# Attention scores as one fp32 product on two row tiles instead of three products of high and low parts

## The chip, the cores and the metric

The kernel runs on one core of a Trainium2 chip, in one launch. The metric is device time in microseconds; the median of the runs of a kernel counts. The engines of the core are named as the profile names them: PE (TensorE matmuls, with its weight loads as PEld), DVE (VectorE), ACT (ScalarE), POOL (GpSimd) and SP (SyncE, which issues the transfers). They run side by side, each works through its own instructions in the order of the program, and semaphores hold an instruction until what it reads is there.

## What is computed

Three parts follow each other: attention in which each query keeps its 32 best keys, a dense two-layer block, and a mixture of eight experts of which each token visits one. The attention has 2 batches, 8 heads, 576 tokens and 64 elements per head. Shortened:

```python
scores = scale * np.matmul(q, k.transpose(0, 1, 3, 2))
kth = np.partition(scores, -top_k, axis=-1)[..., -top_k:-top_k + 1]
scores = np.where(scores >= kth, scores, -1000000000.0)
attn = np.exp(scores - max); attn = attn / (attn.sum + 1e-09)
x = attn @ v                        # then heads side by side: 1152 x 512
h = x @ w_in                        # 512 x 2048, float64 as it comes
x = (h * np.tanh(softplus(h))) @ w_out
expert_idx = argmax(xn @ en.T / tau)
out[mask] = gate_w * (np.maximum(x[mask] @ w1[e], 0.0) @ w2[e])
```

Which 32 keys are kept, and which expert a token visits, hang on comparisons, so the scores must be good to about fp32.

## The kernel before

**Attention** is cut into 36 steps. A step (`attention_step`, p from 0 to 35) takes 128 query rows of two heads (a pair of heads, hp), or, for the last 64 rows of a batch (i = 4, steps 16 to 19), 64 rows of four heads. A step does this, in order: PE transposes the queries (tile pq), ACT copies them to SBUF (qT); PE makes the scores in two halves of 288 keys (tile ps, two units n = 0 and 1, one PSUM buffer of two banks between them), ACT copies each half to sp; DVE finds the 32 largest (eight MAX8 for each row set over 72 keys each into cand, then MAX8 and MATCH_REPLACE8 on cand); ACT counts; DVE or POOL makes the part below (e); DVE takes its maxima; ACT makes exponentials; DVE makes the threshold kths; POOL or DVE masks; PE transposes the masked exponentials (pt) and ACT copies them; PE multiplies with the values (pv); DVE or ACT normalises into x.

**High and low parts.** A query or key is split into two fp32r numbers: the high part is a copy into fp32r (ACT, or POOL by `copy_pool`), the low part is the fp32 number less the high part (POOL, or DVE in batch 0's first pieces). Queries: `queries`, tiles qn and qs. Keys: `keys` for the first 512 keys of a pair of heads (kn, ks; PE transposes the high and the low part, four 128x128 each, into pk), `keys_last` for the last 64 keys (kr, ksr, pkr). All key parts stand in kt, 4 buffers. Scores are then three products, high by high, low by high and high by low (`scores`, L753 to L761): six matmuls of 288 columns per unit. For i < 4 a head's 64 elements lie on 64 of the 128 rows of the array, so the two heads' products use two row tiles. For i = 4 the stationary operand is made block diagonal with zeros (tile qz, POOL memsets at L738 and L739) and has all 128 rows.

**The dense block** (`mixture`) takes the 9 tiles of 128 tokens in five groups, [0], [1, 2], [3, 8], [4, 5] and [6, 7]. For each group: PE transposes x (px), ACT and DVE split it, then eight chunks of hidden features follow (`hidden_chunk`): product with w_in in high and low parts (ph), a chain on ACT and DVE, and full fp32 matmuls of 512 columns with w_out, which add into px2 (`L1137`). The trace shows two instructions for each such fp32 matmul. `route` then picks the expert and scatters the rows to DRAM. The weights come as float64 and are decoded on POOL or ACT and by two DVE instructions a piece (L417, L419), between the attention steps.

**The order** is made when the kernel is built. `Schedule` holds the tasks of all of this with a guessed cost each and plays them through by priority; what it starts first stands first in its engine's program. Priorities are the tables at the top (STEP_AT, GROUP_AT, AT, MT, KS and others); a task with an alternative engine (`alt`) goes to whichever takes it first. Where the plan has PE without work it puts in a pair of filler transposes of the identity (tile spare, L450), which write to nothing that is read.

**The experts** follow when all rows have been scattered: 56 filler transposes (tile idle, L1348), then the loads and products of eight experts, with their own order.

Of the kernel before, what the change touches and what calls it, by code (L numbers as in the profile page):

```python
# [40 lines left out]
SCORE = 0.5  # L41
# [6 lines left out]
NQ = 1  # L48
T_W = 0.3
T_W0 = 10.45  # L50
# [14 lines left out]
TO_POOL = -436.93  # L65
TO_DVE = 366.76
TO_ACT = -391.04
TAIL_ACT = -167.43
COPY_POOL = -619.45
MIN_POOL = -874.77  # L70
SMALL_POOL = -68.14
LOW_POOL = -274.76


STEP_AT = [-690.48, -300.09, -364.55, -131.41, -83.69, 81.75, -47.59, 49.12, 98.53, 207.23, 249.76, 145.44, 276.8, 379.11, 349.13, 518.72, 390.4, 417.55, 459.12, 647.37, 578.05, 722.29, 778.98, 674.46, 841.16, 858.61, 866.0, 892.07, 1181.88, 1269.98, 1300.34, 1344.69, 1451.34, 1775.86, 1867.81, 1605.22]
GROUP_AT = [292.92, 853.45, 992.05, 1761.43, 2294.6]
PACE = [0.0, 0.36, 66.62, 21.19, 0.0]
KEY_AT = [218.94, 98.9, 372.2, 284.11]
KEY_LAST = 117.53
AT = {'scores': [-28.35, -25.88], 'copy': [32.47, -51.62], 'groups': [508.91, 110.67], 'select': [237.28], 'count': [-77.51, 82.96], 'below': [-280.12, 63.52], 'exp': [141.28, -107.06], 'threshold': [-647.59], 'mask': [-230.57, 182.65], 'turn': [31.93, 33.14, -340.91], 'turned': [-759.4, -756.38, -521.2], 'values': [-210.22], 'norm': [-96.66], 'query': [-149.46, -138.7], 'zeros': [-49.59], 'twin': [-766.65], 'load': [-2.3], 'high': [82.4, -1030.81], 'low': [-646.78, -870.83], 'v': [-79.27, 152.95, 385.27], 'number': [46.71]}  # L80
MT = {'add': [-81.29, 169.34], 'exp': [-356.19, -425.7], 'min': [-606.84], 'chain': [-103.69], 'finish': [-121.26], 'out': [354.32], 'turn': [-386.17], 'high': [-481.58], 'low': [-142.53], 'product': [251.93, 118.55]}
RT = [676.11, 267.71, 138.08, 1.49, 303.8, -1157.4, -579.56, -456.58, 307.92, -1338.24]
KS = {'last': [-154.14, -16.09, -762.48], 'load': [107.07], 'tail': [-791.97, -122.26], 'high': [14.75, -375.93], 'low': [463.76, -236.02], 'turn': [416.95, -485.27], 'turned': [-312.48, 363.62]}
WT = {'load': [-589.11], 'tail': [-695.36], 'words': [91.25], 'high': [-432.98], 'low': [-299.85]}
CLEAR_AT = 1140.31
W_FIRST = [-817.47, -87.92, -794.01, -66.65]
# [227 lines left out]
def sparse_attention_mish_moe_kernel(  # L314
# [256 lines left out]
    def lows(eng):  # L571
        return nc.vector if eng == DVE else nc.gpsimd
# [4 lines left out]
    def keys_last(b, pri):  # L577

        kr = mbuf([P, 512], F32, "g", f"kr{b}", 3) if b == 0 else abuf([P, 512], F32, "n", f"kr{b}", 2)
        ksr = abuf([P, 4, 2, P], F32R, "k4", f"ksr{b}", 2)  # L580
        eng = POOL if b else DVE

        def raw():
            return kr.tile[0:64].rearrange("p (h d) -> p h d", h=4)

        t = op(SP, 0.475, pri + KS["last"][0], lambda: nc.sync.dma_start(
            kr.tile[0:64].rearrange("p (h d) -> p h d", h=8), k[b, :, 512:S, :].rearrange("h p d -> p h d")), take=[kr], data=(0.73,))
        t1 = op(ACT, 0.55, pri + KS["last"][1], act(lambda: ksr.tile[0:64, :, 0, :], raw), [t], take=[ksr], use=[kr])
        t2 = op(
            eng, 1.25 if b else 0.6, pri + KS["last"][2],  # L590
            lambda: lows(eng).tensor_tensor(ksr.tile[0:64, :, 1, :], raw(), ksr.tile[0:64, :, 0, :].bitcast(F32), op=ALU.subtract),
            [t1], use=[kr, ksr], port=1.25 if b else 0.6,
        )
        KREM[b] = ksr, t2

    def keys(b, hp, pri, ks_pair=[]):

        eng = POOL if b else DVE
        kn = mbuf([P, 2, 256], F32, "g", f"kn{b}{hp}", 3) if b == 0 else abuf([P, 2, 256], F32, "n", f"kn{b}{hp}", 2)
# [40 lines left out]
        t2 = op(  # L640
            eng, 1.25 if b else 0.6, pri + KS["low"][0], lambda: lo(eng), [t1], use=[kn, ksb],
            alt=None if b else (POOL, 1.25, lambda: lo(POOL), LOW_POOL, 1.25), port=1.25 if b else 0.6,
        )
        for l in range(2):
            pk = bank(f"pk{b}{hp}{l}")

            def transposes(l=l, pk=pk):
# [3 lines left out]
            t3 = op(PE, 0.44, pri + KS["turn"][l], transposes, [t2 if l else t1, tl], take=[pk], use=[ksb])  # L651
            KDONE[b, hp].append(op(
                ACT, 0.5, pri + KS["turned"][l], act(lambda l=l: kt.tile[:, l, 0:512], lambda pk=pk: pk.tile), [t3], use=[pk, kt],
            ))
# [1103 lines left out]
```

## Time and profile before

| | us |
|---|---|
| three runs | 726.35, 727.18, 731.3 |
| median | 727.18 |
| the profiled execution | 732.9 |
| span of its instructions | 731.2 |
| PE busy | 675.2 (92%) |
| DVE busy | 531.3 (73%) |
| ACT busy | 522.4 (71%) |
| POOL busy | 391.3 (54%) |

The span is the time from the first to the last instruction. The rows of a trace give, for each instruction or run of instructions, the start in us from the span's start, the time it took, the engine, the line of the kernel, the operation and out<-in by the kernel's names, with shapes. An instruction of PE is pipelined: its row lasts until its modelled end, so rows overlap, and what a piece of work keeps PE for is read from its start to the start of the next piece. PEclk is the granted clock of TensorE, where 1.00 is 2.4 GHz and 0.50 is 1.2 GHz. A wait in brackets names the engine and the tile that ended it.

### The profile page before, as it was taken

To read this page: it belongs to the slowest core of one execution; us is meant where nothing else is said; L and a number is where in the kernel's file an instruction comes from. 1 tells how busy PE (TensorE), PEld (TensorE's weight loads), DVE (VectorE), ACT (ScalarE), POOL (GpSimd) and SP (SyncE) were. 2 spreads that over 40 slices of the span, in tenths; PEclk is the share of its full clock that TensorE was granted. 3 is DMA by queue.
4 is the path that set the end of the run, shared out by engine and by line. 5 is a ranking of instruction groups with operands and counts; after the bars stand their busy time and mean duration, and the time that the engine had idled before them with its cause. 6 is when DMAs were issued, how large, how long until landed. Compare 5 with 4: busy or idle time off the path is not lost.

```text
span 731.2 us, 15232 instructions
## 1 busy us (share of the span) xinstructions
PE 675.2 (92%) x5412; PEld 530.3 (73%) x5412; DVE 531.3 (73%) x2054; ACT 522.4 (71%) x1105; POOL 391.3 (54%) x360
## 2 busy tenths in 40 slices
PE   7897889887799999999999999999998899999895
PEld 5665676565688775777776787576578899998894
DVE  4789989899888798998788994331126777878741
ACT  4757888888689787788887986665325667777651
POOL 6558777897577766757665573740012242333321
PEclk8778989999899999999999999999998999999998
DMA  8922543330001302000000001330014777776610
GB/s 221 278 72 89 166 133 120 116 103 23 30 1 39 78 1 61 2 30 3 1 3 1 1 31 51 123 130 15 1 46 140 223 228 247 235 233 216 223 39 22
DMA packets 57739, 69.00 MB, mean 94 GB/s; under 512 B 22958, under 2 KB 41390, under 8 KB 57656
## 3 DMA queue, kind: packets, MB, share of 16 engines
q1 hardware_dynamic: 55656, 63.23, 28.4%
q0 software_dynamic: 2000, 4.73, 1.9%
q8 instruction: 44, 0.72, 0.4%
q14 instruction: 39, 0.32, 0.1%
HBM read 60.32 MB, written 8.15 MB: 94 GB/s over the span
## 4 chain that ended last, share of the span: by engine, by line
PE 54%; DMA 12%; DVE 11%; ACT 7%; issue 7%; POOL 7%; POOLq 0%; ACTq 0%; SPq 0%; DVEq 0%
PE px L1137 15%; PE ph L1077 13%; DMA raw<-in_moe_w_dram 7%; PE pt L917 5%; PE ps L761 4%; PE pv L968 4%; PE spare L450 3%; ACT w L1292 2%; DMA out_dram<-yo,ig 2%; DMA raw<-in_moe_w_out_dram 2%; POOL sp L887 2%; DVE t L850 1%; PE pv L963 1%; PE pk L649 1%; POOL w L1260 1%
## 5 line engine op out<-in xcount | busy, mean ns | idle before, releaser
L1137 PE MATMUL px<-w_out_s,g 128*128 128x512 f32 x288 | 140.1, 605 | 0.0
L842 POOL TENSOR_SCALAR e<-sp,t 128x576 f32<-128x576 f32 x45 | 82.0, 1822 | 30.1 <-ACT e L833 27.9
L1260 POOL TENSOR_TENSOR w<-raw,w 128x1024 fp32r<-128x1024 f32 x22 | 53.1, 2425 | 80.5 <-ACT w L1292 62.7
L1077 PE MATMUL ph<-xT,w_in_h 128*128 128x256 f32 x576 | 89.5, 296 | 0.0
L797 DVE MAX8 cand<-sp 128x8 f32<-128x72 f32 x576 | 83.2, 216 | 2.9 <-ACT sp L440 2.9
L1077 PEld LDWEIGHTS ph<-xT,w_in_h 128*128 128x128 f32 x576 | 74.7, 191 | 8.9 <-DVE g L1127 4.3
L440 ACT ACTIVATE pT<-pt 128x512 f32<-128x512 f32 (+1 forms) x108 | 55.1, 519 | 30.3 <-PE pt L923 17.1
L1409 PE MATMUL py<-ht,w 128*128 128x352 f32 x224 | 67.9, 362 | 9.0 <-DVE yT L1436 7.9
L1137 PEld LDWEIGHTS px<-w_out_s,g 128*128 128x128 f32 x288 | 48.4, 190 | 35.8 <-issue 33.1
L1292 ACT ACTIVATE w<-raw 128x1024 fp32r<-128x1024 f32 x56 | 59.1, 1055 | 18.1 <-DMA raw<-in_moe_w_dram 17.7
L887 POOL TENSOR_SCALAR sp<-sp,kths 128x576 f32<-128x576 f32 x32 | 61.2, 1917 | 17.0 <-ACT e L856 5.7
L917 PE MATMUL pt<-ident,e 128*128 128x128 f32 (+1 forms) x360 | 62.1, 294 | 8.4 <-DVE e L890 4.6
L843 POOL TENSOR_TENSOR e<-e,sp 128x576 f32<-128x576 f32 x45 | 66.6, 1479 | 3.8
L917 PEld LDWEIGHTS pt<-ident,e 128*128 128x128 f32 (+1 forms) x360 | 41.9, 143 | 28.3 <-issue 10.9
L450 PE MATMUL spare<-ident 128*128 128x128 f32 x276 | 54.9, 329 | 7.7 <-ACT qT L440 1.9
L856 ACT ACTIVATE e<-sp,t 128x576 f32<-128x576 f32 x72 | 55.1, 772 | 7.7 <-DVE t L850 7.5
L833 ACT ACTIVATE e<-sp,t 128x576 f32<-128x576 f32 x72 | 55.3, 771 | 6.2 <-POOL t L817 3.2
L850 DVE MAX8 t<-e 128x8 f32<-128x576 f32 x72 | 53.5, 750 | 6.7 <-POOL e L843 6.4
L1390 PE MATMUL phe<-xt,w 128*128 128x352 f32 x256 | 57.3, 348 | 0.8 <-DVE xt L1260 0.8
L1410 PE MATMUL py<-ht,w 128*128 128x176 f32 x224 | 54.8, 245 | 0.0
L450 PEld LDWEIGHTS spare<-ident 128*128 128x128 f32 x276 | 34.5, 161 | 25.3 <-PE spare L450 12.0
L1260 DVE TENSOR_TENSOR w<-raw,w 128x1024 fp32r<-128x1024 f32 x42 | 51.1, 1217 | 0.0
(200 smaller groups left out, 1607.7 us busy)
## 6 DMA issues: line engine op xcount, KB each, us to landing
raw<-in_moe_w_dram SPq DMA_DIRECT2D x64, 512.0 KB, 4.1
raw<-in_moe_w_in_dram SPq DMA_DIRECT2D x16, 512.0 KB, 4.8
raw<-in_moe_w_out_dram SPq DMA_DIRECT2D x16, 512.0 KB, 3.3
xs<-zt SPq DMA_DIRECT2D x11, 257.0 KB, 5.1
xe<-xs SPq DMA_DIRECT2D x8, 353.4 KB
qn<-in_q_dram SPq DMA_DIRECT2D x8, 256.0 KB
kn<-in_k_dram SPq DMA_DIRECT2D x8, 256.0 KB
vt<-in_v_dram SPq DMA_DIRECT2D x16, 128.0 KB, 3.2
```

What stands on the lines that cost most here:

```text
L450: nc.tensor.transpose(b.tile[:, j * P:(j + 1) * P], ident, ident)
L797: nc.vector.max(cand.tile[:, o, 8 * g:8 * g + 8], sc[o].tile[:, 72 * g:72 * g + 72])
L842: nc.gpsimd.tensor_scalar(part(o), sc[o].tile, t8b.tile[:, o, 23:24], None, op0=ALU.is_lt)
L843: nc.gpsimd.tensor_tensor(part(o), part(o), sc[o].tile, op=ALU.mult)
L850: (0.67, lambda: nc.vector.max(t8b.tile[:, o, 24:32], part(o))),
L887: nc.gpsimd.tensor_scalar(sc[o].tile, sc[o].tile, kths[:, 2 * p + o:2 * p + o + 1], None, op0=ALU.is_lt)
L917: nc.tensor.matmul(pt.tile[0:c1 - c0, j * P:(j + 1) * P], part(o)[:, c0:c1], ident, is_transpose=True, start=(j == 0), stop=not by_pe[o], ...
L1077: nc.tensor.matmul(d, a, b_, start=(m == 0), stop=(m == len(mm) - 1))
L1137: lambda f=f, f2=f2, ti=ti, x2=x2: nc.tensor.matmul(x2.tile, gt.tile[:, (f2 * n + ti) * P:(f2 * n + ti + 1) * P], w_out_s[:, f, :], start= ...
L1260: eng.tensor_tensor(dst, x, hi.bitcast(F32), op=ALU.subtract)
L1292: nc.scalar.activation(t[:, 0:1024], raw, AF.Copy)
L1409: nc.tensor.matmul(PY[e][d][:, 0:C2], w[:, 0, d * P:(d + 1) * P], ht, start=(f == 0), stop=False)
```

## The change

- `keys_last` and `keys` no longer split. The keys come in as fp32 (kr, kn) and are turned as they are: the last 64 keys by one transpose per pair of heads, the first 512 by eight plain matmuls against the identity, one for each head and 128 keys. Each has 64 columns as its stationary operand and writes 64 partitions of pk, so that the two heads use two column tiles. ACT copies one bank of 512 columns where it copied two. kt is a single fp32 tile of 576 columns.
- `queries` is a load alone (qn, now with two buffers of its own, NQ = 2). A step transposes the queries of its pair by one instruction instead of two.
- `scores` is one fp32 product per head: two matmuls of 288 columns per unit on two row tiles for i < 4. For i = 4 there are four, each on a quarter of the array (64 rows by 64 columns), and the block diagonal tile and its memsets are gone.
- The guessed costs of the new tasks, of the values (1.3 to 1.4) and of the product with w_in (1.42 to 1.46 and 0.93 to 0.95) are new, and so are all priority tables. So the whole order of the program up to the experts is another one.

```diff
-SCORE = 0.5
+SCORE = 0.52
+KTB = 4
-NQ = 1
+NQ = 2
-STEP_AT = [-690.48, -300.09, -364.55, -131.41, -83.69, ...
+STEP_AT = [-652.05, -140.17, 8.92, -270.16, -106.2, ...
...
     def keys_last(b, pri):
...
+        kr = KREM[b] = [abuf([P, 8, D], F32, "kr", f"kr{b}", 1)]
+        kr.append(op(SP, 0.475, pri + KS["last"][0], lambda: nc.sync.dma_start(
+            kr[0].tile[0:64], k[b, :, 512:S, :].rearrange("h p d -> p h d")), take=[kr[0]], data=(0.73,)))
...
         def transpose_last():
-            for l in range(2):
-                nc.tensor.transpose(bl.tile[:, 64 * l:64 * l + 64], ksr.tile[0:64, hp, l].bitcast(F32), ident[0:64, 0:64])
...
-        t1 = op(ACT, 0.57, pri + KS["high"][0], act(lambda: split(0), raw), [t], take=ta, use=[kn, ksb],
-                alt=(POOL, 0.75, lambda: copy_pool(split(0), raw()), COPY_POOL))
-        t2 = op(
-            eng, 1.25 if b else 0.6, pri + KS["low"][0], lambda: lo(eng), [t1], use=[kn, ksb],
...
-                for j in range(4):
-                    nc.tensor.transpose(pk.tile[:, j * P:(j + 1) * P], part()[:, j, l].bitcast(F32), ident)
...
+            nc.tensor.transpose(bl.tile[:, 0:64], kr.tile[0:64, 2 * hp:2 * hp + 2, :], ident[0:64, 0:64])
+
+        def transposes():
+            for j in range(4):
+                for s in range(2):
+                    nc.tensor.matmul(
+                        pk.tile[64 * s:64 * s + 64, j * P:(j + 1) * P], kn.tile[:, s, j, :], ident, start=True, stop=True)
+
+        t3 = op(PE, 0.86, pri + KS["turn"][0], transposes, [t], take=[pk, kt], use=[kn])
+        t4 = op(ACT, 0.59, pri + KS["turned"][0], act(lambda: kt.tile[:, 0:512], lambda: pk.tile), [t3], use=[pk, kt])
...
     def queries(b, i, pri):
...
-            t1 = op(ACT, 0.16 + 0.05 * m, pri + AT["high"][h0 > 0], act(lambda split=split: split(0), raw), [t],
...
-            QDONE[b, i] += [t1] * (m // 2)
+        QDONE[b, i] = [t] * 4
...
         def scores(ps, n):
-            for m, (lq, lk) in enumerate(((0, 0), (1, 0), (0, 1))):
-                for x in range(2):
+            for x in range(2):
+                for s in range(2):
+                    h = slice(64 * s, 64 * s + 64)
                     if i < 4:
-                        h = slice(64 * x, 64 * x + 64)
-                        a, b_ = qT.tile[h, lq], kts[0].tile[h, lk, HB * n:HB * n + HB]
+                        if x == 0:
+                            nc.tensor.matmul(
+                                ps.tile[:, s, 0:HB], qT.tile[h], kts[0].tile[h, HB * n:HB * n + HB], start=True, stop=True)
                     else:
-                        a, b_ = qT.tile[:, n, lq], kts[n].tile[:, lk, HB * x:HB * x + HB]
-                    nc.tensor.matmul(ps.tile[:, x, 0:HB], a, b_, start=(m == 0), stop=(m == 2))
+                        nc.tensor.matmul(
+                            ps.tile[h, x, 0:HB], qT.tile[h, n * 64:n * 64 + 64], kts[n].tile[h, HB * x:HB * x + HB],
+                            start=True, stop=True)
```

Three places of the new order follow. The number after a tile's short name is that of the step, pair of heads or group: ps0_1 is the second unit of step 0, pk00 the keys of batch 0 and pair 0, ph1_0 the first chunk of group 1.

PE from behind the first fillers to the first step's scores, before and then after the change:

```order
L620 MATMUL pkr00_248<-ident_75,ksr0_204 128x64 x2
L620 MATMUL pkr02_254<-ident_75,ksr0_204 128x64 x2
L649 MATMUL pk001_263<-ident_75,ks00_230 128x128 x4
L620 MATMUL pkr01_270<-ident_75,ksr0_204 128x64 x2
L620 MATMUL pkr03_282<-ident_75,ksr0_204 128x64 x2
L727 MATMUL pq0_289<-ident_75,qs00_218 128x128 x2
L727 MATMUL pq2_295<-ident_75,qs00_218 128x128 x2
L649 MATMUL pk000_304<-ident_75,ks00_230 128x128 x4
...
L761 MATMUL ps0_0_317<-kt00_249,qT0_290 128x288 x6
...
L761 MATMUL ps0_1_341<-kt00_249,qT0_290 128x288 x6
```

```order
L659 MATMUL pq0_232<-ident_75,qn00_171 128x128
L659 MATMUL pq3_238<-ident_75,qn00_171 128x128
L604 MATMUL pk00_243<-ident_75,kn00_177 64x128 x8
L599 MATMUL pkr00_257<-ident_75,kr0_122 128x64
L451 MATMUL spare36_263<-ident_75 128x128 x2
L673 MATMUL ps0_0_266<-kt00_244,qT0_233 128x288 x2
L451 MATMUL spare37_274<-ident_75 128x128 x2
L451 MATMUL spare38_278<-ident_75 128x128 x2
L673 MATMUL ps0_1_281<-kt00_244,qT0_233 128x288 x2
```

Nothing but the two query transposes, one pair's keys and its tail stands ahead of the first scores now; all four tails and two pieces of high and low keys stood there.

DVE from the first weight piece to the first group of maxima (cand0), before and then after:

```order
L417 SCALAR_TENSOR_TENSOR w_out_s_101<-raw2_109,w_out_s_101 128x512
L517 SCALAR_TENSOR_TENSOR junk0_210,wsum_95<-w_in_h_99 128x512
L591 TENSOR_TENSOR ksr0_204<-kr0_122,ksr0_204 64x4x128
L696 TENSOR_TENSOR qs00_218<-qn00_135,qs00_218 128x128
L419 SCALAR_TENSOR_TENSOR w_out_s_101<-raw2_109,w_out_s_101 128x512
L517 SCALAR_TENSOR_TENSOR junk2_278,wsum_95<-w_in_h_99 128x512
L636 TENSOR_TENSOR ks00_230<-kn01_252,ks00_230 128x2x4x64
L636 TENSOR_TENSOR ks02_348<-kn02_186,ks02_348 128x2x4x64
L797 MAX cand0_358<-sp0_333 128x8 x16
```

```order
L418 SCALAR_TENSOR_TENSOR w_out_s_101<-raw0_109,w_out_s_101 128x512
L420 SCALAR_TENSOR_TENSOR w_out_s_101<-raw0_109,w_out_s_101 128x512
L418 SCALAR_TENSOR_TENSOR w_out_s_101<-raw3_206,w_out_s_101 128x512
L420 SCALAR_TENSOR_TENSOR w_out_s_101<-raw3_206,w_out_s_101 128x512
L714 MAX cand0_299<-sp0_272 128x8 x16
```

The four subtractions for low parts and two checks of the weights (junk) have left this place, and one more weight piece stands in it.

PE at the first product of group 1 (ph1_0), before and then after:

```order
L1024 MATMUL px2_2812<-ident_75,x02_2323 128x128 x4
L761 MATMUL ps16_0_2817<-kt00_249,qz16_176 128x288 x6
L917 MATMUL pt12_0_2827<-ident_75,e12_2701 128x128 x4
...
L917 MATMUL pt12_2_2853<-ident_75,e12_2701 64x128 x2
...
L1077 MATMUL ph1_0_2858<-xT1_2231,w_in_h_99 128x256 x8
```

```order
L941 MATMUL px2_2638<-ident_75,x02_1898 128x128 x4
L673 MATMUL ps14_1_2652<-kt02_424,qT14_2356 128x288 x2
L659 MATMUL pq18_2656<-ident_75,qn14_2162 128x64 x2
L673 MATMUL ps15_0_2663<-kt03_286,qT15_2635 128x288 x2
L834 MATMUL pt16_0_2676<-ident_75,e16_2541 128x128 x4
...
L834 MATMUL pt16_1_2686<-ident_75,e16_2541 128x128 x4
L994 MATMUL ph1_0_2693<-xT1_2227,w_in_h_99 128x256 x8
```

Group 1 starts behind the values of twelve steps before, and behind those of thirteen after the change; the step whose turned exponentials stand just ahead of it is 12 before and 16 after, which is the fourteenth step in the new order.

## Rows read from the trace of the kernel before

**Rows 1.** Windows: us, busy us of each engine (instructions), clock, DMA share, GB/s.

```profile
0.00:60.00 60.00, 50.44 (x348) 35.02 (x348) 40.09 (x160) 37.50 (x83) 36.80 (x60) 0.80 0.67 191
60.00:200.00 140.00, 115.96 (x1040) 85.17 (x1041) 131.40 (x534) 112.97 (x259) 109.76 (x89) 0.91 0.30 94
200.00:542.00 342.00, 340.07 (x2840) 248.40 (x2840) 237.95 (x1136) 257.57 (x519) 189.46 (x174) 1.00 0.11 31
```

**Rows 2.** Windows of the filler transposes alone: PE and PEld busy, clock, DMA.

```profile
0.00:60.00 60.00, 24.65 (x114) 15.65 (x114) 0.80 0.67 191
60.00:202.00 142.00, 26.76 (x144) 16.69 (x144) 0.92 0.29 93
202.00:542.00 340.00, 3.42 (x18) 2.14 (x18) 1.00 0.11 31
```

**Rows 3.** Timeline of PE: group 1's first product, and the fillers before the experts.

```profile
202.47 1.22 PE L1077 MATMUL ph<-xT,w_in_h 128*128 128x256 f32 x8
...
541.87 6.28 PE L1348 MATMUL idle<-ident 128*128 128x128 f32 x56
```

**Rows 4.** Timeline of DVE, POOL, ACT and PE up to the first maxima.

```profile
9.94 1.46 DVE L591 TENSOR_TENSOR ksr<-kr,ksr 64x512 fp32r<-64x512 f32 x1
11.53 1.75 DVE L419 SCALAR_TENSOR_TENSOR w_out_s<-raw,w_out_s 128x512 int32<-128x512 int32 x1
16.41 0.69 DVE L636 TENSOR_TENSOR ks<-kn,ks 128x512 fp32r<-128x512 f32 x1 [1.74 <-POOL ks L437]
22.89 1.31 DVE L797 MAX8 cand<-sp 128x8 f32<-128x72 f32 x9
```

```profile
10.82 1.91 POOL L636 TENSOR_TENSOR ks<-kn,ks 128x512 fp32r<-128x512 f32 x1
```

```profile
8.82 0.63 ACT L440 ACTIVATE ks<-kn 128x512 fp32r<-128x512 f32 x1
17.48 0.60 ACT L440 ACTIVATE kt<-pk 128x512 fp32r<-128x512 f32 x1 [0.78 <-PE pk L649]
19.68 0.65 ACT L440 ACTIVATE sp<-ps 128x576 f32<-128x576 f32 x1 [1.60 <-PE ps L761]
```

```profile
16.32 1.12 PE L649 MATMUL pk<-ident,ks 128*128 128x128 f32 x4
...
18.55 1.09 PE L761 MATMUL ps<-kt,qT 64*128 64x288 f32 x6
```

**Rows 5.** Timeline of PE in a stretch at full clock, one attention step's pieces among others.

```profile
285.08 0.60 PE L917 MATMUL pt<-ident,e 128*128 128x128 f32 x4
285.52 0.39 PE L923 MATMUL pt<-large,sp 128*128 128x128 bf16 x4
285.74 1.08 PE L1137 MATMUL px<-w_out_s,g 128*128 128x512 f32 x2
286.75 0.45 PE L963 MATMUL pv<-vr,pT 64*64 64x65 f32 x8
287.13 1.16 PE L968 MATMUL pv<-vt,pT 128*64 128x65 f32 x32
288.21 0.66 PE L761 MATMUL ps<-kt,qT 64*128 64x288 f32 x6
288.80 1.12 PE L1137 MATMUL px<-w_out_s,g 128*128 128x512 f32 x2
289.77 0.38 PE L727 MATMUL pq<-ident,qs 128*128 128x128 f32 x2
289.99 1.02 PE L1137 MATMUL px<-w_out_s,g 128*128 128x512 f32 x2
```

**Rows 6.** Chain that ended last: a run of fp32 matmuls on PE.

```profile
464.22 15.45 PE px L1137 x36
```

**Rows 7.** Timeline of PE: a unit with the block diagonal tile, and turned quarters.

```profile
200.30 1.04 PE L761 MATMUL ps<-kt,qz 128*128 128x288 f32 x6
201.18 0.60 PE L917 MATMUL pt<-ident,e 128*128 128x128 f32 x4
...
300.55 1.15 PE L1030 MATMUL px<-ident,xr 64*64 64x64 f32 x32
301.63 0.66 PE L917 MATMUL pt<-ident,e 128*128 128x128 f32 x4
```

**Rows 8.** Groups by line and shape: busy us, mean ns, idle before.

```profile
L847 DVE SCALAR_TENSOR_TENSOR e<-sp,t 128x576 f32<-128x576 f32 x27 | 25.4, 940 | 7.2 <-ACT e L833 7.0
```

More of the change, by code (lines that the diff above doesn't have):

```diff
@@ L77 @@
[L77 to L80, printed above, removed]
@@ new lines @@
+GROUP_AT = [215.39, 643.71, 758.96, 1266.51, 1745.32]
+PACE = [0.36, 14.76, 43.59, 32.28, 0.0]
+KEY_AT = [243.74, 299.51, 86.64, 345.63]
+KEY_LAST = 205.86
+AT = {'scores': [-4.53, -1.8], 'copy': [16.09, 393.84], 'groups': [238.73, 77.91], 'select': [-8.36], 'count': [-113.92, 35.44], 'below': [-470.43, 58.18], 'exp': [36.32, -108.19], 'threshold': [2.33], 'mask': [-591.67, 263.14], 'turn': [16.15, 17.66, 129.19], 'turned': [-225.35, -409.12, -186.17], 'values': [83.13], 'norm': [-190.85], 'query': [-131.82, -95.34], 'zeros': [27.82], 'twin': [-353.52], 'load': [-193.85], 'high': [298.05, -676.92], 'low': [-54.57, -176.97], 'v': [-323.72, -197.51, 345.29], 'number': [-183.36]}
@@ new lines @@
+MT = {'add': [-779.7, 68.54], 'exp': [-168.62, -527.71], 'min': [-518.46], 'chain': [163.71], 'finish': [-244.53], 'out': [210.47], 'turn': [-386.99], 'high': [568.03], 'low': [-111.2], 'product': [140.15, -69.87]}
+RT = [29.74, 243.48, -339.56, -179.03, -260.37, -715.51, -494.7, -493.61, -206.52, -1561.1]
+KS = {'last': [-304.2, -77.22, -561.28], 'load': [-70.6], 'tail': [-309.48, -261.49], 'high': [-64.62, 328.22], 'low': [-443.95, 598.69], 'turn': [134.18, -606.25], 'turned': [-536.43, 748.69]}
@@ L87 @@
+WT = {'load': [-1030.47], 'tail': [-382.3], 'words': [-53.38], 'high': [-601.81], 'low': [-489.44]}
+CLEAR_AT = 191.31
+W_FIRST = [-246.86, -56.35, -610.59, -209.41]
 LATENCY = {PE: 0.2, ACT: 0.04, DVE: 0.04, POOL: 0.05, SP: 2.0}
@@ L577, in keys_last @@
     def keys_last(b, pri):
[L579 to L587, printed above, removed]
@@ L588, in keys_last @@
-        t1 = op(ACT, 0.55, pri + KS["last"][1], act(lambda: ksr.tile[0:64, :, 0, :], raw), [t], take=[ksr], use=[kr])
-        t2 = op(
[L590 to L599, printed above, removed]
+        kr = KREM[b] = [abuf([P, 8, D], F32, "kr", f"kr{b}", 1)]
@@ L640, in keys @@
-        t2 = op(
-            eng, 1.25 if b else 0.6, pri + KS["low"][0], lambda: lo(eng), [t1], use=[kn, ksb],
[L642 to L647, printed above, removed]
-                for j in range(4):
-                    nc.tensor.transpose(pk.tile[:, j * P:(j + 1) * P], part()[:, j, l].bitcast(F32), ident)
[L651 to L654, printed above, removed]
+        kr, krt = KREM[b]
@@ L1080, in hidden_chunk @@
         t1 = [
-            op(PE, 0.93 if n == 1 else 1.42, pri + MT["product"][f2], lambda f2=f2: product(f2), split + wd, take=[] if f2 else [ph], use=[ph, xT], share=0.75 if n == 1 else 1.0)
+            op(PE, 0.95 if n == 1 else 1.46, pri + MT["product"][f2], lambda f2=f2: product(f2), split + wd, take=[] if f2 else [ph], use=[ph, xT], share=0.75 if n == 1 else 1.0)
             for f2 in range(2)
```

113 lines of the change are left out of this document (30 added, 83 removed).

## The prediction

> **What bounds the kernel now.** I read the windows first, by stages. From 60 to 200 us DVE is busy for 131.4 of 140 us, while PE's 116 us hold many fillers [rows 1]. So I asked for the windows of the fillers alone: 24.7 us before 60, 26.8 us from there to 202, and 3.4 us in the 340 us after that, all of these at the very end [rows 2]. Up to about 202 us attention on DVE sets the pace and PE has time to spare; from then on PE is busy for 340.1 of 342 us at full clock [rows 1]. The timeline of PE shows what lies at the border: at 202.47 the first product of group 1 of the dense block starts, and from there PE never runs dry until it reaches the fillers ahead of the experts at 541.87 [rows 3]. The time is therefore a sum of three: **t1** = 202.5 us until group 1 starts, set by DVE; **R** = 541.9 - 202.5 = 339.4 us of PE work behind that start; **P2** = 731.2 - 541.9 = 189.3 us for the experts, whose code does not change. The profiled execution took 732.9 us, 1.7 beside the span, and the median of the runs shown is 727.2, 5.7 less. I make the sum on the profiled one and take the difference off the median.
>
> **The change in t1: the start.** DVE's first maxima start at 22.89 [rows 4]. They wait for a chain: high parts of the keys on ACT at 8.82, low parts on POOL until 12.73, transposes of both, copies (17.48), scores at 18.55, their copy at 19.68, then the second unit. In the new order only pq0, pq3, pk00 and one tail stand ahead of the first scores, and they need loads alone. The split at 8.82 shows that the first keys had landed by then. They are now issued behind the values of pair 0, 0.29 MB more at the 191 GB/s of this stretch [rows 1]: 1.5 us, so 10.3. The eight key products are sixteen instructions in pairs, 1.12 us for each four turns at this clock [rows 4], so some 1.9 us, and I take 12.2; copy 0.6, tail and its copy 0.5: first scores at 13.3. A unit of scores here takes 1.1 us and its copy 0.65 [rows 4], and the second unit must wait for the first one's copy, since they share a buffer: 13.3 + 2 x 1.75 = 16.8. The extra weight piece ahead of the maxima on DVE costs 2 x 0.7, and its load should be there by then. So the first maxima start near 16.5 instead of 22.9: **-6.4 us**. The bounds are -6.4 and 0; it is lost if DVE idles for as much later. DVE's work up to group 1 doesn't shrink by itself: the order has the same steps in it and one more, and eight of the comparisons go from POOL to DVE for the whole kernel, 8 x 0.94 = 7.5 us [rows 8], against the low parts, checks and small operations that leave it. I count these as even, by the groups' means.
>
> **The change in t1: POOL's shadow on DVE.** While POOL subtracts low parts (10.82 to 12.73), DVE's 64x512 subtraction takes 1.46 us and a weight word 1.75, where a 128x512 subtraction takes 0.69 at 16.41 with POOL quiet [rows 4]. That is 0.8 and 1.1 us lost beside one POOL subtraction of 1.9 us. The order before has eight such subtractions on POOL ahead of group 1, two of them in the start just counted; the new one has none. Six that cost DVE nothing bound this at 0, six at 0.7 each at 4; of the operations that then stand on DVE these two are the only kind that I see stretched, so I take a value near the lower end, **-1.5 us**.
>
> **The change in R.** I count what stands behind group 1's first product in each order and price it at full clock. Query transposes, 44 before and 19 after: 0.22 us for two [rows 5], -2.7. Values, 24 steps before and 23 after: 286.75 to 288.21 [rows 5], -1.5. Turned exponentials, 234 before and 222 after at 0.11, and their mask products, 70 and 56 at 0.055 [rows 5]: -1.3 and -0.8. Key turns, 32 and 24 at 0.11: -0.9; tails, 8 and 3: -0.3. Sum -7.5. The scores go the other way. Before: 33 units of two row tiles at 0.59 (288.21 to 288.80 [rows 5]) and 8 block diagonal ones at 0.88 [rows 7], 26.5 us. After: 35 and 4. An fp32 matmul of 512 columns is two instructions of 15.45 / 36 = 0.429 us [rows 6]; 288 columns make 0.241. If the two heads' matmuls run side by side, a unit is 2 x 0.241 = 0.48. To this comes the cost of going in and out of row tiles: today's unit is three pairs of 288 columns at half an fp32 instruction's time, 0.36, and takes 0.59, so 0.23. A unit costs 0.71, one of i = 4 has four such passes and costs 0.97 + 0.23 = 1.20: 35 x 0.71 + 4 x 1.20 = 29.7, **+3.2**. Keys turned in column tiles pay the 0.23 too, three sets behind group 1: +0.7. In all R changes by -7.5 + 3.2 + 0.7 = **-3.6 us**. Bounds: no cost of going in and out would make the scores 20.7 (R -13); matmuls in turn, with no overlap, make a unit 0.97 + 0.23 = 1.20 and one of i = 4 2.16, 50.6 us (R +17). I take the overlap: the values, fp32 on two column tiles, need 40 instructions in 1.46 us [rows 5], 0.037 each, while 65 columns at the rate of [rows 6] are 0.054; and the quarter turns, fp32 on two row and two column tiles, take 32 in 1.08 us [rows 7], 0.034 where 64 columns in turn are 0.054.
>
> Two rules of the Trainium skill speak against this change. TensorEngine Tiling, section Key Properties, says that a change of the tiling mode drains the engine; the 0.23 us agree with it, and by that rule the key turns and the quarter units pay what the whole-array ones did not, which is the 0.7 above and part of the 3.2. The same page, section Restrictions and Gotchas, says that different row tiles cannot use one PSUM bank at the same time; a unit of i = 4 does just that (both heads write bank x). The quarter turns into px do it too, and overlap, so the trace does not bear it out here.
>
> As a mechanism of this kernel, passes that take turns in one bank would make the four quarter units behind group 1 cost 2.16 each: +3.8, 719.5 us. I give that 1 in 20, inside the forecast's range. By the second of the two rules it would come out so.
>
> **Sum.** -6.4 - 1.5 - 3.6 = -11.5 on the profiled execution: 721.4, and 727.2 - 11.5 = 715.7 for the median; I say 715.5. P2 is left as it is: its loads of expert weights and its splits are issued in the same order, with the same engines.
>
> **Rivals.** *The early gain doesn't last.* DVE has no less to do before group 1, and it was 94% busy from 60 to 200 [rows 1]; if it runs out of ready steps for 8 us more on the way, t1 stays and only R's -3.6 is left: 723.6, within 1%. For it speaks that each step is a long chain over five engines; against it that ACT and POOL, which release DVE's waits, both lose work. Chance 0.21. *The row tiles take turns in fp32.* Then R gets 50.6 - 29.7 = 20.9 us more, and the time is 736, slower. The place is each unit of scores behind group 1; it decides against the change once a unit costs 11.5 / 43 = 0.27 us more than I think (quarter units counted twice). Units before t1 would hide in 51 us of fillers [rows 2]. Against it stand the overlaps above; that none of them is fp32 on two row tiles with full columns leaves it a chance of 0.09. *DVE gains more.* With POOL freer, DVE's stretching falls by its upper bound (2.5 us more), and DVE's idle time up to 202 us, some 30 us, shrinks by a fifth as ACT and POOL have less in their queues (6 us more): 707. Chance 0.10.
>
> **How the numbers follow.** The forecast, 710 to 720.5, has 0.60. A measurement of this kernel can tell about 1% from no change: 719.9 is the border. Faster gets the forecast and the third rival and a little less for the forecast's edge: 0.70. Same: the first rival and that edge, 0.21. Slower: the second, 0.09. The range leaves out the second rival and half of the third: 707 to 725.
>
> **What would show it.** In the profile after: first maxima near 16.5 us instead of 22.9; group 1's first product at 194 to 196; from there to the fillers ahead of the experts about 336 us with PE full; a unit of scores 0.7 us long, its two heads starting together; P2 at 189. I am wrong if a unit takes 1.2, if PE runs dry after group 1 has started, or if group 1 starts at 202 in spite of an earlier first maximum.

## The result and the profile after

The kernel after takes 719.51 us (median of 717.2, 718.75, 720.28 and 720.57) against 728.95 of before beside it: the ratio is 0.987, with a 95% interval of 0.982 to 0.992. In a second comparison, on the chip of a part of the experiments, it was 717.6 against 727.8, ratio 0.982 (0.977 to 0.987). Some executions of either kernel were over 1.5% longer than the fastest beside them and are left out here and below. The 9 other runs of after have the median 718.45 together, the 53 of before 727.8: **9.4 us less**. The forecast was 715.5, 11.7 less than the median that was shown then.

The windows of the profiled execution (span 717.0, 718.75 us with what lies around it) answer to [rows 1] and, for the fillers alone, to [rows 2]. Columns as there: us, busy us of PE, PEld, DVE, ACT and POOL with their instructions, clock, DMA share, GB/s.

```profile
0.00:60.00 60.00, 47.73 (x417) 32.89 (x418) 48.71 (x221) 41.04 (x93) 38.37 (x62) 0.97 0.72 209
60.00:190.00 130.00, 109.53 (x982) 74.86 (x982) 121.46 (x504) 108.52 (x260) 89.61 (x74) 0.93 0.29 94
190.00:524.00 334.00, 332.07 (x2663) 229.85 (x2661) 226.00 (x1090) 242.34 (x489) 147.97 (x145) 1.00 0.11 32
524.00:717.00 193.00, 170.11 (x1188) 163.24 (x1188) 123.17 (x232) 114.62 (x244) 56.06 (x39) 0.94 0.57 174
```

```profile
0.00:60.00 60.00, 20.59 (x120) 15.07 (x120) 0.97 0.72 209
60.00:190.00 130.00, 13.75 (x78) 8.03 (x78) 0.93 0.29 94
190.00:524.00 334.00, 3.00 (x16) 1.93 (x16) 1.00 0.11 32
```

The picture is the one of before: DVE at 93% up to 190 us with fillers on PE, then PE at 332 of 334 us. DVE is busy for 48.7 us of the first 60, where it was 40.1. The two borders, in the timeline of PE, answer to [rows 3]:

```profile
189.91 1.20 PE L994 MATMUL ph<-xT,w_in_h 128*128 128x256 f32 x8
...
523.97 6.33 PE L1265 MATMUL idle<-ident 128*128 128x128 f32 x56
```

So t1 went from 202.47 to 189.91, R from 339.40 to 334.06, and P2, whose code is the same, from 189.3 to 193.0. The start, in the timelines of PE and of DVE, answers to [rows 4]:

```profile
9.14 0.41 PE L659 MATMUL pq<-ident,qn 128*128 128x128 f32 x2 [0.19 <-DMA qn<-in_q_dram]
11.46 1.09 PE L604 MATMUL pk<-ident,kn 128*64 128x128 f32 x16 [1.91 <-ACT qT L441]
...
13.62 0.76 PE L673 MATMUL ps<-kt,qT 64*128 64x288 f32 x4
...
15.13 0.76 PE L673 MATMUL ps<-kt,qT 64*128 64x288 f32 x4 [0.16 <-ACT sp L441]
```

```profile
15.35 0.63 DVE L714 MAX8 cand<-sp 128x8 f32<-128x72 f32 x4
16.62 1.58 DVE L714 MAX8 cand<-sp 128x8 f32<-128x72 f32 x11 [0.64 <-ACT sp L441]
```

And two units of scores behind group 1's start, one of i < 4 and one of i = 4, with the pieces that follow them (they answer to the units in [rows 5, 7]):

```profile
205.30 1.19 PE L676 MATMUL ps<-kt,qT 64*64 64x288 f32 x8
206.42 1.13 PE L1054 MATMUL px<-w_out_s,g 128*128 128x512 f32 x2
...
291.07 0.76 PE L673 MATMUL ps<-kt,qT 64*128 64x288 f32 x4
291.76 1.22 PE L994 MATMUL ph<-xT,w_in_h 128*128 128x256 f32 x8
```

From start to next start a unit keeps PE for 0.69 us and one of i = 4 for 1.12.

### The profile page after: what moved, and what is told of

Its sections match the earlier page's. It is cut to its first block, busy times and chain, and to the rows that moved or that the text cites. A ratio compares the mean times of both kernels' runs of the same rounds, so it can differ in the third digit from the quotient of the medians.

```text
span 717.0 us, 14819 instructions
## 1 busy us (share of the span) xinstructions
PE 659.4 (92%) x5244; PEld 500.8 (70%) x5244; DVE 519.3 (72%) x2044; ACT 506.5 (71%) x1084; POOL 332.0 (46%) x319
## 3 DMA queue, kind: packets, MB, share of 16 engines
q1 hardware_dynamic: 55656, 63.23, 29.2%
## 4 chain that ended last, share of the span: by engine, by line
PE 50%; DMA 15%; DVE 14%; ACT 9%; issue 7%; POOL 3%; POOLq 0%; SPq 0%; ACTq 0%; DVEq 0%
PE px L1054 15%; PE ph L994 12%; DMA raw<-in_moe_w_dram 8%; PE pv L885 5%; PE pt L834 4%; PE ps L673 4%; DMA out_dram<-yo,ig 2%; DVE cand L714 2%; DVE t L767 2%; PE pv L880 2%; ACT w L1209 2%; DVE w_out_s L418 1%; PE phe L1307 1%; DMA raw<-in_moe_w_in_dram 1%; ACT e L750 1%
## 5 line engine op out<-in xcount | busy, mean ns | idle before, releaser
L1054 PE MATMUL px<-w_out_s,g 128*128 128x512 f32 x288 | 142.9, 612 | 0.0
L994 PEld LDWEIGHTS ph<-xT,w_in_h 128*128 128x128 f32 x576 | 75.0, 191 | 12.4 <-issue 5.2
L759 POOL TENSOR_SCALAR e<-sp,t 128x576 f32<-128x576 f32 x37 | 66.3, 1791 | 32.2 <-ACT e L750 26.7
L441 ACT ACTIVATE pT<-pt 128x512 f32<-128x512 f32 (+1 forms) x108 | 53.6, 519 | 27.6 <-PE pt L840 14.1
L834 PE MATMUL pt<-ident,e 128*128 128x128 f32 (+1 forms) x360 | 58.7, 283 | 8.0 <-DVE e L807 3.9
L834 PEld LDWEIGHTS pt<-ident,e 128*128 128x128 f32 (+1 forms) x360 | 39.3, 137 | 33.0 <-issue 16.4
L804 POOL TENSOR_SCALAR sp<-sp,kths 128x576 f32<-128x576 f32 x30 | 56.3, 1879 | 10.5 <-DVE t L787 8.3
L760 POOL TENSOR_TENSOR e<-e,sp 128x576 f32<-128x576 f32 x37 | 54.3, 1467 | 3.1
L673 PE MATMUL ps<-kt,qT 64*128 64x288 f32 x256 | 49.7, 464 | 3.0 <-ACT sp L441 2.9
L441 ACT ACTIVATE sp<-ps 128x576 f32<-128x576 f32 x72 | 46.4, 644 | 8.5 <-PE ps L673 7.4
L1326 PEld LDWEIGHTS py<-ht,w 128*128 128x128 f32 x224 | 43.0, 192 | 13.3 <-DVE yT L1353 5.4
```

What stands on the lines that cost most here:

```text
L441: return lambda: nc.scalar.activation(out(), in_(), func, **kw)
L673: nc.tensor.matmul(ps.tile[:, s, 0:HB], qT.tile[h], kts[0].tile[h, HB * n:HB * n + HB], start=True, stop=True)
L759: nc.gpsimd.tensor_scalar(part(o), sc[o].tile, t8b.tile[:, o, 23:24], None, op0=ALU.is_lt)
L834: nc.tensor.matmul(pt.tile[0:c1 - c0, j * P:(j + 1) * P], part(o)[:, c0:c1], ident, is_transpose=True, start=(j == 0), stop=not by_pe[o], ...
L994: nc.tensor.matmul(d, a, b_, start=(m == 0), stop=(m == len(mm) - 1))
L1054: lambda f=f, f2=f2, ti=ti, x2=x2: nc.tensor.matmul(x2.tile, gt.tile[:, (f2 * n + ti) * P:(f2 * n + ti + 1) * P], w_out_s[:, f, :], start= ...
```

## The experiments

All are compared by the same three stretches. Each row is one profiled execution; the medians are of all the kernel's runs. "First maxima" is DVE's first MAX8, "clock" the granted clock of the first 100 us.

| kernel | median | first maxima | t1 | R | P2 | clock |
|---|---|---|---|---|---|---|
| before | 727.8 | 22.89 | 202.5 | 339.4 | 189.3 | 0.83 |
| before again | | 23.47 | 198.7 | 339.8 | 188.1 | 0.91 |
| after | 718.45 | 15.35 | 189.9 | 334.1 | 193.0 | 0.98 |
| after again | | 16.77 | 191.5 | 335.3 | 189.1 | 0.97 |
| old tables | 742.2 | 13.74 | 207.5 | 348.9 | 188.0 | 0.81 |
| scores twice, late | 738.8 | 16.01 | 199.3 | 354.2 | 191.5 | 0.90 |
| scores twice, early | 724.7 | 16.88 | 199.5 | 334.7 | 191.9 | 0.91 |
| maxima twice | 737.0 | 16.25 | 212.9 | 334.9 | 188.4 | 0.90 |
| late start | 723.2 | 19.72 | 196.5 | 334.0 | 193.4 | 0.95 |
| fp32r scores | 713.3 | 16.36 | 202.4 | 322.2 | 186.3 | 0.75 |
| three transposes a filler | 717.0 | 15.93 | 191.1 | 334.1 | 188.9 | 0.98 |
| both of these | 700.7 | 15.57 | 191.1 | 322.5 | 184.5 | 0.95 |
| POOL twice | 731.4 | 16.92 | 208.4 | 333.6 | 189.2 | 0.88 |

R repeats to 1.7 us wherever the work behind group 1 is the same; t1 moves by 4 between two executions of before, and by more in a case below. P2, with the same code in each row, lies between 188.0 and 193.4, but for the two fp32r rows, whose scores are rounded (186.3 and 184.5).

### The two kernels again

> The kernel after itself, unchanged, for a second profile and more times beside the experiments. In the other three profiled runs of the new order the granted clock fell to 0.66 in the stretch from 10 to 20 us where after's profile has 1.00, and their first maxima came 0.7 to 1.5 us later. If that is chance from run to run, this profile may show it too: group 1's start between 190 and 196, R 334 (within 1), and the experts 188 to 193. If the experts took 193 because of the change, they take 193 again; if by chance, 188 to 191 as in the three others.

> The kernel before itself, for a second profile. If what was read from one execution holds, group 1 starts at 202 to 206, R is 339 (within 1), the experts 187 to 193, and first maxima start near 22.9. If the clock at the start is chance here too, the granted clock between 10 and 20 us is another than 0.58.

After again: t1 191.5, R 335.3 (a little above what was expected), P2 189.1, and the clock from 10 to 20 us was 0.66 where the first profile of after had 1.00. So the 193.0 of the experts was chance, and after's clock at the start is too. Before again: first maxima 23.47, t1 198.7 (3.3 below what was expected), R 339.8; its clock from 10 to 20 us was 0.58 again, so for before no chance shows there. Over the two executions of each, t1 falls by 9.9 (200.6 to 190.7), R by 4.9 (339.6 to 334.7).

### Before's tables on after's operations

The tables of priorities at the top of the file (T_W to W_FIRST) are before's, as the diff of the change lists them; nothing else is edited.

> After's operations with before's priority tables (the guessed costs stay after's): separates what the removed and added operations do from what the new order does. If the gain is that of the operations, as the prediction's sum has it (keys and queries need no split ahead of the first scores, less PE work behind group 1), the time is 715 to 722, like after's 719.5. If the gain is that of an order tuned to the new operations, it is as long as before or longer, 727 to 740, with PE's work behind group 1 no longer than after's but idle time or fillers in it, or group 1 starting near 200.

742.2 us (738.5 to 746.2), 13 to 14 more than before. The first maxima come earliest of all, at 13.74, and yet group 1 starts at 207.5. In R there are 348.9 us: five units of scores more stand behind group 1's start than in after (192 score instructions against 172), and 355 turned exponentials and mask products against 278. So the operations don't make the gain in before's tables, and an early start alone doesn't either. That is the mechanism of the first rival, in another order than the one forecast. The reverse, before's operations with tables made anew for them, was not tried; how much of the gain is due to the operations and how much to new tables is open.

### Score products twice, behind and ahead of group 1

```diff
-            for x in range(2):
+            for x in [0, 1] * (2 if p not in EARLY else 1):
```

EARLY is the set of steps 0 to 12. The early version has `p in EARLY`.

> After, with every score product of steps 13 to 35 made twice into the same place (38 units, and 8 units of i = 4). About 35 units and 4 of i = 4 of these stand behind group 1's start. Theory (PE is the bound there, and the two heads' passes run side by side): 35 x 0.46 + 4 x 0.9 = 19.7 us more, R 353, time about 738. Rival, passes take turns: twice as much, some 39 us, time 758. Rival, PE isn't what bounds this stage: below 8 us more.

> After, with every score product of steps 0 to 12 made twice (26 units of i < 4, 26 x 0.46 = 12.0 us of PE), nearly all ahead of group 1's start. Theory (DVE sets the pace there and PE fills its spare time with fillers): 0 to 4 us more, the chain of the first step included. Rival, PE's work on the way of each step to DVE counts there too: 8 to 12 us more.

Late: 738.8, 20.3 more than after. A doubled unit in the timeline of PE is one run of eight instructions:

```profile
292.90 1.24 PE L674 MATMUL ps<-kt,qT 64*128 64x288 f32 x8
```

R rose by 20.1 over the first profile of after, from start to next start the scores in it by 20.8 (28.5 to 49.3); the theory had 19.7. PE's time behind group 1 goes one to one into the result, and two passes of 288 fp32 columns for each head cost 0.48 together (a unit went from 0.69 to 1.17), not 4 x 0.24: the second rival, turn by turn, is excluded. The profiled execution took 746.6 where the other four took 738.5 to 738.9; its group 1 started 9 us later than after's, of which over 5 arise in the first 90 us, in code that is still after's. So t1 of a single profile can be off by that much.

Early: 724.7, 6.3 more, for 26 x 0.48 = 12.5 us of PE at full clock. That is between the two expectations. PE's work ahead of group 1 isn't free, though fillers stand beside it: about half of it arrives. The profile's clock is lower too (0.91 in the first 100 us, after's 0.97 and 0.98), and I can't tell the two apart.

### Maxima twice

```diff
-            for g in range(8):
+            for g in list(range(8)) * (2 if o == 0 and p < 13 else 1):
```

> After, with the first eight maxima of each of the steps 0 to 12 made twice on DVE: some 13 x 1.1 = 14 us more of DVE ahead of group 1's start. Theory (DVE's work sets t1): group 1 starts 11 to 14 us later, near 202, and the time is 730 to 734. Rival (the wait for PE, ACT and POOL sets t1, with DVE idle in between): 0 to 5 us more.

737.0, 18.6 more. The 104 maxima more keep DVE for 13.7 us (0.13 each, start to start), and t1 rose by 21.4 over after's repetition. DVE sets t1, as the theory says, but more was lost than was added. In the same stretch the small operations `t<-t` took 5.8 us instead of 1.6 and others a little more: shifted against POOL, they were held (see below).

### A late start

```diff
         def transposes():
+            for _ in range(40 if (b, hp) == (0, 0) else 0):
+                nc.tensor.transpose(pk.tile[:, 0:P], ident, ident)
```

> After, with 40 identity transposes on PE ahead of the turns of the first keys, 40 x 0.11 = 4.4 us (more at half the clock), so that the first scores and the first maxima start that much later, near 20. Theory (the start is on the path: what the first maxima gain, group 1's start gains): group 1's start and the time 3 to 5 us later, 723 to 725. Rival (DVE's later idle time takes it up, so the early maxima by themselves are worth nothing): 0 to 1 us, 720.

723.2, 4.8 more (715.2 to 725.7), and t1 at 196.5, 5.0 to 6.6 later, for first maxima 2.9 to 4.4 later. That is what the theory expects. But the four times overlap with after's (712.3 to 720.6), and a single t1 can be off by 5, so it is likely, and not shown, that the start is on the path in this order.

### Scores in fp32r, and the clock

```diff
-        kt = KT[b, hp] = abuf([P, S], F32, "kt", f"kt{b}{hp}", KTB)
+        kt = KT[b, hp] = abuf([P, S], F32R, "kt", f"kt{b}{hp}", KTB)
...
-        qT = abuf([P, P], F32, "qT", f"qT{p}", 2)
+        qT = abuf([P, P], F32R, "qT", f"qT{p}", 2)
...
```

> After, with queries and keys rounded to fp32r as they are copied, and one fp32r product per head in place of the fp32 one for i < 4 (so the low parts are left out of the scores); the units of i = 4 stay in fp32. A unit has one pass of 288 columns per head instead of two, so about 0.7 - 0.24 = 0.46 us. Theory (PE bound behind group 1): 35 units x 0.24 = 8.4 us less there, R 326, and little ahead of it: 709 to 713. Rival (the cost of a unit is its switch into row tiles, not its columns): 0 to 3 us less.

713.3 us, 5.1 less than after. R fell by 12.4, more than was expected: a unit is down from 0.69 to 0.33, since one fp32r pass of 288 columns, 0.13 from start to next start, stands for two fp32 ones of 0.24, where I had taken out just one of 0.24 (three fp32r passes and 0.20 make before's 0.59). 35 x 0.36 = 12.6. But group 1 started at 202.4, 11 to 12.5 later than in after, which the expectation did not have. The windows of PE show a lower clock there (us, PE busy, clock, DMA share, GB/s; first after again, then fp32r):

```profile
0.00:100.00 100.00, 78.80 (x718) 0.97 0.60 176
100.00:190.00 90.00, 75.52 (x664) 0.92 0.26 80
```

```profile
0.00:100.00 100.00, 80.26 (x607) 0.75 0.59 165
100.00:190.00 90.00, 76.80 (x615) 0.86 0.28 89
```

Three kernels tested whether the clock is what was lost. In the first the scores of steps 0 to 12 were made twice in the fp32r version (the edit as above). In the others each filler has three transposes:

```diff
-            for j in range(NDUM):
+            for j in range(NDUM + 1):
```

> The fp32r version (low parts left out of the scores of i < 4) with the products of steps 0 to 12 made twice, so that PE has about as much score work ahead of group 1 as after, while behind it the short units stay. In the fp32r version R fell by 12 us, but group 1 started at 202, 11 later than after, with a granted clock of 0.75 in the first 100 us (0.98 in after's profile). Theory (fewer columns on PE ahead of group 1 make the clock fall there, and this lengthens every step's chain): the clock in the first 100 us goes back up to 0.9 or more, group 1 starts at 191 to 196, R stays 322, time 702 to 707. Rival (the clock fell for another reason, or isn't what delays group 1): group 1 at 198 to 204, time 711 to 716.

> After, with three transposes in each filler instead of two (their cost in the plan too little by one transpose, so the order is after's). Some 100 fillers ahead of group 1 give 100 x 0.11 = 11 us more of PE there. Theory (a clock that doesn't fall helps the steps ahead of group 1 more than the fillers delay them): clock 0.97 or more up to 190 us, group 1 at 186 to 190, time 713 to 717. Rival (fillers stand in the way of the steps' own work): group 1 at 193 to 200, time 721 to 728.

> The fp32r version (low parts left out of the scores of i < 4) with three transposes in each filler instead of two. Theory (the clock is what the fp32r version lost ahead of group 1): clock in the first 100 us 0.9 or more instead of 0.75, group 1 at 190 to 196, time 700 to 707. Rival: group 1 stays at 198 to 204, time 711 to 716.

The fp32r version with its early scores twice takes 702.3 (699.2 to 705.9), 11 less than without them: more work, and a shorter time. The mean clock over the span is 0.958 to 0.963 in these runs, and 0.924 to 0.946 without the second products; there is no profile among them, so group 1's start is not known. With three transposes a filler the fp32r version takes 700.7; the windows and the borders:

```profile
0.00:100.00 100.00, 81.70 (x778) 0.95 0.61 178
100.00:190.00 90.00, 78.11 (x648) 0.87 0.24 78
```

```profile
191.08 1.18 PE L994 MATMUL ph<-xT,w_in_h 128*128 128x256 f32 x8
...
513.61 6.33 PE L1265 MATMUL idle<-ident 128*128 128x128 f32 x56
```

The clock of the first 100 us is back at 0.95, t1 at 191.1, and R stays at 322.5. So idle matmuls between the steps' own can be worth 11 us of t1, and PE work that is saved ahead of group 1 can be paid back in clock. In after, whose clock is at 0.97 there anyway, the third transpose changes nothing that can be told: 717.0 against 718.45, t1 191.1, between the two expectations. No kernel that computes the scores in full was seen to beat after.

### POOL twice

```diff
-        t3 = op(POOL, 1.5, pri + WT["low"][0], lambda: nc.gpsimd.tensor_tensor(lo, full, hi.bitcast(F32), op=ALU.subtract), [t2], port=1.5)
+        t3 = op(POOL, 1.5, pri + WT["low"][0], lambda: [nc.gpsimd.tensor_tensor(lo, full, hi.bitcast(F32), op=ALU.subtract) for _ in range(2)], [t2], port=1.5)
```

> After, with POOL's subtraction of the weights' low parts (w_in_l, 1.42 us each) made twice for all sixteen pieces, all ahead of group 1: 22.7 us more of POOL there. It prices the shadow of POOL on DVE by itself: by the prediction's six subtractions at 0 to 0.7 us each, sixteen cost DVE 0 to 11 us; at its value of 0.25 each, 4 us. Theory: group 1's start and the time 3 to 5 us later, 722 to 724. Rival (no shadow worth naming, and POOL has time to spare): 0 to 1 us. Above 8 us: the shadow is as long as the bound, or steps wait for POOL itself.

731.4 us, 12.9 more than after, and t1 at 208.4: above the 8 us that I had named. DVE did the same work, and was kept for it 180.4 us instead of 168.0 in after again (from each start to the next start or its own end), 0.8 us for each of the sixteen subtractions. Its weight words, grouped by line up to t1 (busy us, mean ns, idle before), after again and POOL twice:

```profile
L418 DVE SCALAR_TENSOR_TENSOR w_out_s<-raw,w_out_s 128x512 int32<-128x512 int32 x32 | 24.7, 776 | 11.1 <-ACT w_out_s L416 6.5 <-POOL w_out_s L415 4.6
L420 DVE SCALAR_TENSOR_TENSOR w_out_s<-raw,w_out_s 128x512 int32<-128x512 int32 x32 | 24.6, 775 | 0.1
```

```profile
L418 DVE SCALAR_TENSOR_TENSOR w_out_s<-raw,w_out_s 128x512 int32<-128x512 int32 x32 | 30.2, 950 | 9.9 <-POOL w_out_s L415 5.2 <-ACT w_out_s L416 4.7
L420 DVE SCALAR_TENSOR_TENSOR w_out_s<-raw,w_out_s 128x512 int32<-128x512 int32 x32 | 27.7, 874 | 0.1
```

The rest of t1's 17 us is idle time of DVE (28.0 instead of 23.5), some of which goes with the lower clock (0.88 and 0.87 in the two stretches). Little of it is waiting for POOL's results: those waits went from 8.4 to 9.6 us, while the waits for PE's pv and ACT's e went from 2.7 to 7.5. More than that I haven't told apart.

## Why the prediction was right, and where not

**The stages and their bounds** hold. R behaves as PE's sum (scores twice: 20.1 for 19.7 expected), t1 moves with DVE's work (maxima twice) and, as far as one profile tells, with the start (late start). That units of scores ahead of t1 hide in the fillers does not hold: about half of the early products arrived.

**R: -3.6 forecast, -4.9 measured** on two executions of each. What PE is kept for behind group 1's first product, from start to next start, in the first profile of each:

| us | before | after | change | forecast |
|---|---|---|---|---|
| query transposes | 5.1 | 2.2 | -2.9 | -2.7 |
| values | 35.1 | 33.6 | -1.5 | -1.5 |
| exponentials and masks | 33.7 | 31.5 | -2.2 | -2.1 |
| key turns and tails | 5.0 | 3.7 | -1.3 | -0.5 |
| scores | 26.8 | 28.5 | +1.7 | +3.2 |

After's counts were right to the instruction (35 and 4 units), of before's units 34 and 7 stand there and not 33 and 8, and the two heads' passes run side by side. What stands in no row, code that isn't changed, makes 0.9 more, and R's -5.3 in this pair. The scores' term was too large by 1.5: a unit of i < 4 takes 0.69 (0.71 forecast; its cost beyond the passes is 0.20, not 0.23), one of i = 4 1.12 (1.20), and before's were 26.8 instead of 26.5. A set of sixteen key products takes 1.03, which is 0.15 more than eight pairs of its middle at 0.11: 0.5 for three sets, where I had put 0.7. Before's four turns took 0.49, where I had put 0.44.

A unit of i = 4 has four passes of two row tiles that write one PSUM bank pairwise, and takes 1.12, where passes in turn would need 8 x 0.24 = 1.9. The rule of the Trainium skill, TensorEngine Tiling, section Restrictions and Gotchas, that different row tiles cannot use one bank at the same time, does not show here; the measurement decides.

**The start: -6.4 forecast.** The first maxima came 7.5 earlier in the first pair of profiles and 6.7 in the second, by the steps that were named: first scores at 13.62 (13.3), a second unit behind the first one's copy. That it lasts is likely by the late start's t1, but its times do not show it. Group 1's first product came at 189.9 and 191.5, ahead of the 194 to 196 that were named as a sign. DVE's idle time up to t1, which was 29.2 and 25.3 us in the two executions of before and is 19.8 and 23.5 in those of after, fell by 5.6 in the mean, 4.9 of it in the first 50 us.

**POOL's shadow: -1.5 forecast, and this is the term that was mis-sized.** What DVE is kept for up to t1 fell from 173.4 to 169.1 (means of two), 4.3 us, although after has a step more in it. The forecast counted DVE's work as even, and said that the subtraction and the weight words are the only kind that is seen stretched. Neither holds. Priced at the mean of each group, after's counts are 3.2 us more, and its instructions are 7.5 us shorter. The two groups of small operations `t<-io_f,t` and `t<-t` alone are 7.6 shorter, and the weight words are 1.7 longer. In the groups by line up to t1, before and then after again:

```profile
L870 DVE SCALAR_TENSOR_TENSOR t<-io_f,t 128x8 f32<-128x8 f32 x26 | 8.2, 349 | 0.0
L863 DVE TENSOR_SCALAR t<-t 128x2 f32<-128x2 f32 x13 | 7.2, 553 | 0.8 <-ACT e L833 0.8
L517 DVE SCALAR_TENSOR_TENSOR junk<-w_in_h 128x512 f32<-128x512 f32 x2 | 2.5, 1227 | 0.7 <-ACT w_in_h L536 0.7
...
L1184 DVE TENSOR_TENSOR acc<-acc,sm 128x8 f32<-128x8 f32 x1 | 1.3, 1300 | 0.0
```

```profile
L787 DVE SCALAR_TENSOR_TENSOR t<-io_f,t 128x8 f32<-128x8 f32 x28 | 5.1, 218 | 0.0
L780 DVE TENSOR_SCALAR t<-t 128x2 f32<-128x2 f32 x11 | 3.6, 330 | 0.9 <-ACT e L750 0.7
L518 DVE SCALAR_TENSOR_TENSOR junk<-w_in_h 128x512 f32<-128x512 f32 x1 | 0.7, 684 | 0.0
L1101 DVE TENSOR_TENSOR acc<-acc,sm 128x8 f32<-128x8 f32 x1 | 0.2, 167 | 0.0
```

An operation on 128 x 2 numbers took 553 ns in the mean, one on 128 x 8 1300. The timelines of POOL and DVE in before show how:

```profile
65.76 1.56 POOL L843 TENSOR_TENSOR e<-e,sp 128x576 f32<-128x576 f32 x1
67.28 1.26 POOL L538 TENSOR_TENSOR w_in_l<-w_out_s,w_in_h 128x512 fp32r<-128x512 f32 x1
...
130.04 2.56 POOL L842 TENSOR_SCALAR e<-sp,t 128x576 f32<-128x576 f32 x1
```

```profile
65.97 1.37 DVE L863 TENSOR_SCALAR t<-t 128x2 f32<-128x2 f32 x1
67.26 1.90 DVE L847 SCALAR_TENSOR_TENSOR e<-sp,t 128x576 f32<-128x576 f32 x1
...
131.89 0.14 DVE L863 TENSOR_SCALAR t<-t 128x2 f32<-128x2 f32 x1
```

The small operation starts 0.2 us behind POOL's and ends with it (67.34 and 67.32); the next one is still at it 0.6 us behind the end of POOL's next (69.16 and 68.54). By the Trainium skill, SBUF — State Buffer, section Who interferes with whom, DVE and POOL share a pair of ports, and a DVE instruction that needs it (one with two inputs in SBUF, or in a mode that uses two ports) is blocked until a POOL instruction that came first is done. The first pair agrees, if the small operation runs in such a mode, which no row tells; in the second DVE's row starts 0.02 us ahead of POOL's, too close to say which came first. Not every small operation is held: at 131.89 the same one took 0.14 us in the middle of a POOL operation. So the price hangs on what stands beside POOL's operation, and it goes up to nearly that operation's whole length: 0.8 us in the mean for each of those that were doubled.

With this price the six subtractions that the forecast counted behind the start are worth 4.7, not 1.5. The trace of before has nine ahead of 202.47, not eight, and seven behind the start. DVE's instructions beside these seven took 4.9 us longer than the shortest of their shape take, and 4.0 in before again (an estimate). The price belongs to an order, not to the operations alone: in the old tables the subtractions are gone too, and DVE is still kept for 173.4 us up to t1. There POOL makes 18 of the comparisons in that time, where before makes 13 and after 12.

**Sum.** By the profiles t1 and R fell by 14.8, which is more than the 11.5 forecast, and the spans by 12.5 (means of two each). The medians of all runs fell by 9.4, which is less. Some of the difference is the clock of the executions that were profiled: before's two had mean clocks of 0.954 and 0.964 over the whole span (0.964 is the mean of its 49 runs with a clock on record), after's 0.969 and 0.971 (0.967 in its 9). By the slope below that is an estimated 1.5 and 0.9 us. What remains, some 1 us in the spans, is no more than the runs scatter. With R's 4.9 taken as certain, the typical run has 4 to 5 us left for t1 and P2 together, against 7.9 forecast; so a part of the early gain may well be lost again in most runs, as the first rival has it. How the 4 to 5 divide between start, shadow and clock I can't tell, since runs without a profile don't show t1. That the total came within 2.3 us of the forecast is in part luck: R fell by 1.3 more than forecast, and t1 and P2 together by some 3 less.

**P2** is unchanged, as forecast, as far as its scatter tells: 188.0 to 193.4 over the eleven profiles that compute the scores in full.

## What to carry to other kernels

Where a vector engine sets the pace, removing work from POOL can pay too, and adding it can cost (23 us more of it cost 12.9 here): look for tiny operations with a mean of hundreds of ns, and find what ran on POOL beside them. Where PE sets the pace, count instructions behind the border and price them from start to next start; that part of the sum was good to 2 us. And before crediting PE work that is saved where PE isn't the bound, look at the granted clock of that stretch, which may take the gain back.

## What the hardware showed that was not expected

- **Runs at a lower clock are longer.** Of 49 runs of before, the quarter with the lowest mean clock (0.954) took 731.5 us in the mean, the quarter with the highest (0.973) 726.0: about 3 us for 0.01. By itself that does not show which of the two makes the other. From 200 to 520 us the clock is 0.99 or 1.00 in every profile; it differs in the first 200 us and in the experts, with the same program.
- **Less work on PE took longer.** The fp32r scores ran at 0.75 in the first 100 us, and with more idle transposes at 0.95, and the kernel was 12.6 us faster with them.
- **An operation of a few numbers on DVE can take as long as the POOL operation beside it**, 1.37 us for 128 x 2, where it takes 0.14 when it is not held.
- **A unit of scores in row tiles costs 0.20 us beyond its passes.** Inside a unit the pairs start 0.24 us after one another in fp32 and 0.13 in fp32r; the first and the last pair take 0.1 more each. So a unit of one fp32r pass takes 0.33, one of three 0.59, one of two fp32 passes 0.69. The whole-array units of before pay such a 0.1 only at their first pass (0.22 to 0.24, then 0.13), in seven of their eight.
